# First feed-forward layer, token blocks 3 to 6: the first product as seven quarter products of 256 columns, with the work recorded and issued by a table of shifts

## The chip, the cores and the metric

The kernel runs on one core of a Trainium2 chip. The metric is the device time of one execution in microseconds (us); of several runs the median is given. The engines are named as in the profile: PE multiplies matrices, PEld is PE's loading of weights, DVE and ACT are the vector and the scalar engine, SP issues the DMAs.

## What is computed

Chunked attention over 4 sequences of 768 tokens and 8 heads of 64 gives 3072 rows of 512 numbers; two feed-forward layers follow. All of it is float32.

```python
# attention, per chunk of 32 tokens (8 memory tokens, 16 to the left, 8 to the right)
a = np.exp(scores - max);  out = (a / sum) @ v_full
x = out.transpose(0, 2, 1, 3).reshape(3072, 512)
h = np.maximum(x @ moe_w_in, 0.0)                 # 512 -> 2048
x = h * h @ moe_w_out                             # 2048 -> 512
h = x @ moe2_w_in                                 # 512 -> 2048
return (np.maximum(h, 0) + np.log1p(np.exp(-np.abs(h)))) @ moe2_w_out
```

## The kernel before

Every float32 operand of a large product is held as two parts, a high one (`xh`, `wh`, `gh`) and a low one (`xl`, `wl`, `gl`), and each product is three matmuls: low weights by high data, high by low, high by high.

The 3072 tokens are six blocks of 512 columns (`NB`; the code counts them from 0, the text from 1). The 2048 hidden units are 16 chunks of 128 (`KF`, index `f`); two chunks make a pair (`KP` = 8 pairs, index `p`). The program has three parts.

- **The head** (`FIRST`, an order written out by hand): loads, the attention of block 1, the splitting of the first layer's weights and block 1 of the first layer.
- **Blocks 2 to 6 of the first layer**: `step(n, f)`, called in the order of `n` and `f`. A step runs `h_mm` (12 matmuls of 512 columns into the PSUM tile `hp`: four pieces of the 512-long inner dimension by three parts), then `g_step` (ACT: relu, square, cast to `gh`; the low part `gl` follows on DVE, `act1_low`, at the next step), and `out_step` for a chunk two steps older (12 matmuls of 512 columns into the four accumulators `acc`). At the block's end `evac` copies the accumulators out and stores them (`x2s`). `x_split` makes `xh` and `xl` of the next block with four casts and four subtractions.
- **The second layer**: the blocks taken two at a time (`NGR` = 3 groups of 1024 tokens). Its first product is already made of seven products for every pair of weight chunks (`first_stage`), its second one is `second_stage`. Weights for it are prepared beforehand and kept in DRAM (`wa`, `wb`, `wo`).

Beside the matmuls, the steps of blocks 2 to 5 carry two other kinds of work. The attention of the next block is done in four pairs of units (`p_scores`, `p_exp`, `p_norm`, `p_squares`, `p_values`, `p_out`): short matmuls on PE, the softmax on DVE and ACT, 16 transposes of 32x32 tiles per pair of units on DVE. And `jobs2` splits the second layer's weights: `in_jobs` (load, join two 32-bit halves, four sums or differences, casts, stores to `wa` and `wb`) and `out_jobs` (the same without sums, to `wo`), one job per step.

All engines take their instructions in the order of the program, which here is the order in which the code is written (`tc.manual_schedule()`); SP's DMAs too stand in one queue in that order. A tile that is written anew waits for the last reader of what it held.

The lines of the before kernel that the prediction names:

```python
for a, b in ...:  matmul(out=hp, ...)         # L331, L332, L333: first product, three parts
nc.tensor.matmul(out=acc[m][:, cols], ...)    # L379: second product
nc.vector.transpose(pt[...], t[...])          # L240: transposes of the attention
nc.vector.tensor_tensor(out=o, in0=a, ...)    # L486: sums of second-layer weights, 256 columns
```

L278 and L171 are the attention's short matmuls, L309 makes `xl`, L355 makes `gl`, L436 and L437 join the halves of a second-layer weight, L294 is `p_out`'s copy out of PSUM, L343, L347 and L351 are relu, square and cast, L113 is the scaling of a weight's upper half, L423 is `store` (`wa`, `wb`).

Of the kernel before, what the change touches and what calls it, by code (L numbers as in the profile page):

```python
# [1 line left out]

# [30 lines left out]
UC = 2  # L33
# [12 lines left out]
NGR = NB // 2  # L46
SOFT_A = ((), (0,), (1,), (2, 3), (4,), (5,), (6, 7), ())
# [8 lines left out]
sc2 wb3 wd0 re1 wh0 mx2 cp0 wl2 wp0 vl4 mu1 wa3 va0 vl5 wd3 vl6 tr1 sb2 vl7 wh3 xh1 sc3 wp3 kl8 xh0 ex2 xl1 kl9 xl0  # L56
cp1 su2 va1 mx3 re2 xh2 sb3 wa1 mu2 ex3 wl3 wb1 tr2 xl2 xh3 su3 cp2 xl3 f10 wd1 re3 wh1 va2 mu3 wa2 wb5 wp1 tr3 xh5
cp3 xl5 wb2 xh4 va3 wd2 vl10 xl4 sc4 xh6 wl4 ra0 xl6 xh7 wh2 xl7 f11 wl5 wp2 vl9 mx4 wa5 f12 kl12 wb4 wa4 vl8 wd5
rb0 sb4 wh5 wd4 ra1 rc0 f13 wh4 ex4 wl6 wp4 rb1 kl10 su4 ra2 wb6 rb2 re4 wa6 rl0 f14 mu4 rc1 wd6 rc2 wa7 wb8 wh6 tr4
rl1 wb7 f20 cp4 wl7 wp6 kl11 ra3 vl11 wp5 va4 wa9 rl2 wa8 f21 wd7 rb3 wd8 f15 ra4 rb4 wb10 wh8 wb9 wb11 wh7 wl8 wd9  # L60
f22 wp8 wh9 xo9 xo8 wp7 rc3 wp9 wa10 sc5 rl3 rc4 wd10 f23 ra5 wa11 rl4 mx5 rb5 wd11 wh10 f24 sb5 wl9 wh11 wp10 ex5
wl10 wa12 su5 f16 wb12 re5 wd12 mu5 wh12 wb13 f17 ra6 wp11 wl11 wp12 wa14 tr5 wb14 f18 ra7 wd14 cp5 rb7 wa13 va5 rb6
wd13 rc7 vl14 f19 rc5 kl13 wh13 rl5 wb15 ra8 wl12 wp13 rc6 f25 xo10 xo11 rl6 wh14 ra9 wa15 sc6 f26 kl17 mx6 vl12
wd15 wl13 vl15 kl16 sb6 wh15 wp14 f110 rb8 wl14 wa16 vl13 rl7 kl14 kl15 ex6 rc8 f27 wa17 wb17 wb16 ra10 su6 rb10
f111 wd16 rl8 wh16 re6 wp15 rb9 f28 rc9 wd17 wa18 mu6 wb18 f112 rl9 wd18 wp16 tr6 f29 cp6 ra11 wh18 rb11 wp18 va6
rc11 f113 vl17 xo13 rc10 wl15 ra12 rl10 wh17 xo12 f210 wp17 rb12 sc7 wa19 f114 ra13 kl19 mx7 rc12 vl16 sb7 kl18 rl12
rl11 f115 wb19 ra14 rb13 wd19 rb14 wh19 f211 ra15 rc13 ex7 rl13 su7 f212 wp19 re7 mu7 tr7 f116 cp7 va7 ra16 rc14
f213 xo15 rl14 xo14 rb16 rb15 rc16 f214 rc15 rl15 rl16
# [3 lines left out]


@with_exitstack
def body(ctx: ExitStack, tc: tile.TileContext, qk, vW, w1, w2, out):
    nc = tc.nc
# [20 lines left out]
    raw, cf, wt = {}, {}, {}  # L97
# [31 lines left out]
    def w_h(layer, i, m=BOTH):  # L129
        if (layer, i) not in wt:  # L130
            t = wpool.tile([P, 2, 2, DM], F32R, tag=f"w{i}", name=f"w{layer}_{i}")
            wt[layer, i] = t[:, 0], t[:, 1]
        return nc.scalar.copy(out=wt[layer, i][0][:, m], in_=cf[layer, i, m.start])
# [45 lines left out]
    def p_max(n):  # L179
# [10 lines left out]
        m = at.tile([P, 2, PU * 2, 1], F32, tag="m", name="m", bufs=2)  # L190
# [41 lines left out]
    def p_squares(n, i):  # L232
# [137 lines left out]
    def out_mm(f, g, cols=ALL):  # L370
        gh, gl = g
        wh, wl = (a[:, 1] for a in wt[1, f])
        if f == 0 and cols.start == 0:
            for m in range(4):
                acc[m] = pa.tile([P, DM], F32, tag=f"acc{m}", name=f"acc{m}")
        for m in range(4):
            s = slice(m * P, (m + 1) * P)
            for j, (a, b) in enumerate(((wl[:, s], gh), (wh[:, s], gh), (wh[:, s], gl))):
# [22 lines left out]
    qk_s = wpool.tile([P, PU, NP, GQ + NK], F32, tag=f"w{KF - 1}", name="qk_s")  # L401
    v_s = wpool.tile([P, 2 * PU, UC, 2, 2, D], F32, tag=f"w{KF - 2}", name="v_s")
# [16 lines left out]
    wb = [dram.tile([P, 3, 2, QW], F32R, name=f"wb{p}") for p in range(KP)]  # L419
    wo = [dram.tile([P, 2, 2, DM], F32R, name=f"wo{p}") for p in range(KP)]  # L420
# [37 lines left out]

    def in_jobs(p):
# [13 lines left out]
        def split(k, x, *stores):  # L473
            t = cf_tile(k, (P, 2, 2, QW), F32R)
            halves(t[:, :, 0], t[:, :, 1], x, *[(o, t[:, i]) for o, i in stores], late=True)

        def sums():
            f = d["f"].rearrange("p i (h q) -> p i h q", h=2)
            s = d["s"] = cf_tile(0, (P, 4, QW))
            for out, a, b, op in (  # L480
                (s[:, 0], f[:, 1, 0], f[:, 1, 1], ALU.add),
                (s[:, 1], s[:, 0], f[:, 0, 0], ALU.subtract),
                (s[:, 2], f[:, 0, 1], s[:, 1], ALU.subtract),
                (s[:, 3], f[:, 0, 0], f[:, 1, 0], ALU.subtract),
            ):
                nc.vector.tensor_tensor(out=out, in0=a, in1=b, op=op)  # L486
# [8 lines left out]
        def at(fn, *a):  # L495
            return lambda: fn(*a)
# [390 lines left out]
```

## Time and profile before

| | |
|---|---|
| median of 3 runs | 1094.7 us (1093.49 to 1098.32) |
| the profiled execution | 1093.54 us |
| its span | 1091.7 us |
| granted TensorE clock | 1.00 throughout |
| PE busy | 1075.2 us (98% of the span) |
| PEld busy | 886.6 us (81%) |
| DVE busy | 709.3 us (65%) |
| ACT busy | 594.8 us (54%) |

The profiled execution's time is 1.8 us more than its span, the time from the first to the last instruction. PE's matmuls are pipelined, so a start-to-start distance, not the length of a record, says what one costs in a row.

### The profile page before, as it was taken

What the parts mean: (1) busy time and instruction counts of PE and PEld (TensorE: products, weight loads), DVE (VectorE), ACT (ScalarE), POOL (GpSimd) and SP (SyncE); (2) the same over time, 40 slices, a digit from 0 to 9 for tenths busy, and PEclk for the clock granted to TensorE, in tenths of its full rate; (3) what the DMA queues carried; (4) which work ended last, traced back from release to release, by engine and by line L of the source; (5) the groups of instructions that cost most, each with busy time, mean ns of one, the idle gap of its engine ahead of it and who ended that gap; (6) DMA issues with size and microseconds to landing.
All of it is one profiled execution on the core that took longest, in us unless ns stands there. A gap on an engine that the chain in (4) does not pass through costs nothing.

```text
span 1091.7 us, 18550 instructions
## 1 busy us (share of the span) xinstructions
PE 1075.2 (98%) x7592; PEld 886.6 (81%) x7592; DVE 709.3 (65%) x1175; ACT 594.8 (54%) x926; POOL 0.7 (0%) x6
## 2 busy tenths in 40 slices
PE   5999999999999999999999999999999999999998
PEld 4888888888888888888888888888888888888886
DVE  6876576666667665764332788952788952788822
ACT  3876444454454554546445767732767732767522
POOL 0000000000000000000000000000000000000000
PEclk9999999999999999999999999999999999999999
DMA  9774242354445254534512656234556334555202
GB/s 354 276 281 155 90 165 103 124 202 155 152 160 181 98 176 162 183 113 157 181 39 93 239 189 257 99 126 150 185 183 258 111 118 154 183 187 219 77 1 77
DMA packets 49428, 174.99 MB, mean 160 GB/s; under 512 B 5312, under 2 KB 5312, under 8 KB 41152
## 3 DMA queue, kind: packets, MB, share of 16 engines
q1 hardware_dynamic: 49344, 173.82, 45.2%
q8 instruction: 59, 0.97, 0.4%
q14 instruction: 25, 0.20, 0.1%
HBM read 138.15 MB, written 35.65 MB: 159 GB/s over the span
## 4 chain that ended last, share of the span: by engine, by line
PE 95%; DMA 2%; DVE 1%; ACT 1%; issue 0%; SPq 0%; ACTq 0%
PE acc L379 23%; PE bk L807 23%; PE bk L724 21%; PE hp L331 8%; PE hp L332 8%; PE hp L333 8%; PE xs L278 1%; DMA qk<-qk 1%; PE xs L171 1%; PE xp L278 1%; DMA x2f<-x2s 1%; PE sc L171 1%; DMA r<-w 1%; PE xpe L278 0%; PE pp L254 0%
## 5 line engine op out<-in xcount | busy, mean ns | idle before, releaser
L379 PE MATMUL acc<-gh,w 128*128 128x512 f32 (+1 forms) x776 | 238.1, 388 | 0.0
L807 PE MATMUL bk<-ws,gh 128*128 128x512 f32 x768 | 236.5, 389 | 0.0
L724 PE MATMUL bk<-xo,ws 128*128 128x512 f32 x1008 | 230.2, 389 | 0.0
L724 PEld LDWEIGHTS bk<-xo,ws 128*128 128x128 f32 x1008 | 189.0, 188 | 39.9 <-DVE h L768 0.8
L379 PEld LDWEIGHTS acc<-gh,w 128*128 128x128 f32 x776 | 144.5, 188 | 29.8
L807 PEld LDWEIGHTS bk<-ws,gh 128*128 128x128 f32 x768 | 144.2, 188 | 30.1
L331 PE MATMUL hp<-xh,w 128*128 128x512 f32 (+1 forms) x388 | 153.3, 395 | 0.0
L332 PE MATMUL hp<-xl,w 128*128 128x512 f32 (+1 forms) x388 | 151.0, 389 | 0.0
L333 PE MATMUL hp<-xh,w 128*128 128x512 f32 (+1 forms) x388 | 150.9, 389 | 0.0
L379 PE MATMUL acc<-gl,w 128*128 128x512 f32 (+1 forms) x388 | 150.1, 387 | 0.0
L807 PE MATMUL bk<-ws,gl 128*128 128x512 f32 x384 | 149.5, 389 | 0.2 <-DVE gl L444 0.2
L355 DVE TENSOR_TENSOR gl<-r,gh 128x512 fp32r<-128x512 f32 (+1 forms) x97 | 66.2, 684 | 97.2 <-ACT gh L351 96.8
L444 DVE TENSOR_TENSOR gl<-h,gh 128x512 fp32r<-128x512 f32 x96 | 66.1, 689 | 83.7 <-ACT gh L449 83.4
L449 ACT CAST gh<-h 128x512 fp32r<-128x512 f32 x96 | 59.3, 621 | 106.9 <-PE bk L807 106.7
L343 ACT ACTIVATE r<-hp 128x512 f32<-128x512 f32 (+1 forms) x97 | 57.4, 592 | 105.3 <-PE hp L333 99.9
L331 PEld LDWEIGHTS hp<-xh,w 128*128 128x128 f32 x388 | 73.4, 189 | 15.7
L333 PEld LDWEIGHTS hp<-xh,w 128*128 128x128 f32 x388 | 73.4, 189 | 15.1
L332 PEld LDWEIGHTS hp<-xl,w 128*128 128x128 f32 x388 | 73.4, 189 | 14.4 <-DVE xl L321 0.2
L379 PEld LDWEIGHTS acc<-gl,w 128*128 128x128 f32 x388 | 72.8, 188 | 14.8
L807 PEld LDWEIGHTS bk<-ws,gl 128*128 128x128 f32 x384 | 72.1, 188 | 15.6 <-DVE gl L444 0.8
L240 DVE STREAM_TRANSPOSE pt<-t 32x128 f32<-32x128 f32 x256 | 77.5, 303 | 4.3
L347 ACT ACTIVATE r<-r 128x512 f32<-128x512 f32 (+1 forms) x97 | 60.8, 629 | 2.6
(79 smaller groups left out, 1087.9 us busy)
## 6 DMA issues: line engine op xcount, KB each, us to landing
ws<-wa SPq DMA_DIRECT2D x24, 1024.0 KB, 6.4
ws<-wo SPq DMA_DIRECT2D x24, 1024.0 KB, 4.9
ws<-wb SPq DMA_DIRECT2D x24, 768.0 KB, 4.3
r<-w SPq DMA_DIRECT2D x16, 1024.0 KB, 7.2
cf<-w SPq DMA_DIRECT2D x32, 512.0 KB, 5.3
qk<-qk SPq DMA_DIRECT2D x46, 336.0 KB, 5.4
v<-vW SPq DMA_DIRECT2D x44, 256.0 KB, 5.3
wo<-cf SPq DMA_DIRECT2D x16, 512.0 KB, 2.9
```

Source lines behind the costliest of these rows:

```text
L240: nc.vector.transpose(pt[b:b + 32, g], t[g * 32:(g + 1) * 32, i, h])
L331: nc.tensor.matmul(out=hp, lhsT=b, rhs=xh[:, c], start=(c == 0), stop=False)
L332: nc.tensor.matmul(out=hp, lhsT=a, rhs=xl[:, c], start=False, stop=False)
L333: nc.tensor.matmul(out=hp, lhsT=a, rhs=xh[:, c], start=False, stop=(c == KD - 1))
L343: nc.scalar.activation(out=r, in_=hp, func=AF.Relu)
L347: nc.scalar.activation(out=r, in_=r, func=AF.Square)
L355: nc.vector.tensor_tensor(out=gl, in0=r, in1=gh.bitcast(F32), op=ALU.subtract)
L379: nc.tensor.matmul(out=acc[m][:, cols], lhsT=a, rhs=b, start=(f == 0 and j == 0 and cols.start == 0), stop=(f == KF - 1 and j == 2),)
L444: nc.vector.tensor_tensor(out=lo, in0=x, in1=hi.bitcast(F32), op=ALU.subtract)
L449: nc.scalar.copy(out=hi, in_=x)
L724: nc.tensor.matmul(out=bk, lhsT=a, rhs=b, start=(start and n == 0), stop=(n == 5), skip_group_check=not start)
L807: nc.tensor.matmul(out=bk, lhsT=a, rhs=b, start=(f == 0 and j == 0), stop=(f == KF - 1 and j == 2))
```

## The change

In blocks 3 to 6 (code `n` = 2 to 5) the first product of a pair of chunks takes the form that the second layer has. The block's 512 columns are two halves of 256, the inner dimension is two halves, the pair of chunks is two; instead of eight products of such quarters there are seven, of sums and differences of the quarters. A product (`quarter`) is 6 matmuls of 256 columns. So a pair takes 7 x 6 = 42 matmuls of 256 columns where it took 24 of 512.

What this needs:

- **Weights.** `sum_jobs` makes, in block 2, four sums of the first layer's weights for each pair, splits them and stores them in DRAM (`wx`, 8 x 4 x 256 KB). `sum_load` brings each of the four back into a fixed place in SBUF once for every pair and block (tiles named `w_9`, `w_11`, `w_13`, `w_15`), after its last reader.
- **Data.** `octet` makes four differences and seven split parts (`xe`, and two in the tiles `w_1` to `w_7`) of each block, where `x_split` made four parts.
- **PSUM.** A pair has one tile `hq` with two halves `e` and `a`. Seven results pass through them and are put together in SBUF (`r`) by four ACT copies and three DVE additions of 256 columns per pair, where ACT read `hp` directly. Relu, square, cast and low part stay.
- **Place of the jobs.** `jobs1` (the sums) take `in_jobs`' place in block 2; `in_jobs` go to blocks 3 to 5, `out_jobs` to block 6, where the data for the second layer (`x_jobs`) is made too.
- **Buffers.** `qk` has 2 buffers instead of 4, `m` and `s` one each. The head's loads of `qk` stand elsewhere in `FIRST`. The second layer's first weights (`ws`) go to other places, and the last two `out_step`s stand behind the first two products of the second layer.
- **Order.** From block 2 to the second pair of the second layer nothing is issued as the code is written. A `Recorder` keeps every instruction; `play` puts each DMA, DVE and ACT instruction at its place among PE's instructions, moved by a number from the table `MOVES`, and issues all in that order. Where two tiles share a buffer, `play` adds a dependency so that they take it in the order of issue.

```diff
+MOVES = (
+    """
+19 34 39 2 8 17 -56 -8 -56 3 22 26 28 30 33 40 45 49 34 41 46 50 -42 -45 1 4 3 7 3 6 3 6 -1 1 4 10 11 18 23 27 12 20
...
+    def play(self, moves):
+        jobs, self.jobs = self.jobs, None
...
+            if engine is self.nc.tensor:
+                order.append((at + 0.5, i))
+                at += 1
+            else:
+                order.append((at + int(next(moves, 0)), i))
+        for _, i in sorted(order):
...
-            t = at.tile([P, NP, GQ + NK], F32, tag="qk", name="qk", bufs=2 * PU)
+            t = at.tile([P, NP, GQ + NK], F32, tag="qk", name="qk", bufs=PU)
...
+        def words():
+            f = d["f"] = cf_tile(ka)
+            for i in range(2):
+                hi, lo = (a[:, 0].bitcast(F32) for a in wt[1, 2 * p + i])
+                nc.vector.tensor_tensor(out=f[:, i], in0=hi, in1=lo, op=ALU.add)
...
+        def casts():
+            split(kc, d["s"][:, 0:2], (wx[p][:, 0:2], slice(0, 2)))
+            split(ka, d["s"][:, 2:4], (wx[p][:, 2:4], slice(0, 2)))
...
+        def sum_place(i):
+            return whole[9 + 2 * i][:, :, 0, 0:QW]
+
+        def sum_load(p, i):
+            store(sum_place(i), wx[p % KP][:, i])
...
+        def quarter(x, w, bk, start):
+            n = 0
+            for k in range(2):
+                wh, wl = (w[:, h, k * P:(k + 1) * P] for h in range(2))
+                for a, b in ((wl, x[0][:, k]), (wh, x[1][:, k]), (wh, x[0][:, k])):
+                    nc.tensor.matmul(out=bk, lhsT=a, rhs=b, start=(start and n == 0), stop=(n == 5), skip_group_check=not start)
...
+            if old:
+                on, op, oe, oa, or0, or1 = old
+                quarter(xp_o[on, 2], sum_place(1), oa, False)
+                quarter(xp_o[on, 3], sum_place(2), oe, False)
+                if here:
+                    for i in (1, 2):
+                        sum_load(op + 1, i)
+            outs(1)
+            if old:
+                nc.scalar.copy(out=or0[:, half[1]], in_=oa)
+                nc.vector.tensor_tensor(out=or0[:, half[1]], in0=oe, in1=or0[:, half[1]], op=ALU.add)
+                nc.scalar.activation(out=or0, in_=or0, func=AF.Relu)
+            if here:
+                bk = ps.tile([P, BLK], F32, tag="ps", name="hq")
+                e, a = bk[:, half[0]], bk[:, half[1]]
+                quarter(xp_o[n, 4], whole[2 * p][:, :, 0, QW:], e, True)
...
+                quarter(xp_o[on, 5], sum_place(3), oa, False)
...
-            for n in range(1, NB):
-                for f in range(KF):
-                    step(n, f)
+            for f in range(KF):
+                step(f)
...
+            for n in range(2, NB):
+                for p in range(KP):
+                    slot(n, p)
```

A pair's work is spread over three calls of `slot`: the first product of quarters and two more in its own, three in the next (`old`), the last one there too, and its relu, square and second product in the next and the one after it. Recorded instructions all carry the line L157, so the rows below are told apart by their tiles.

**PE, in a middle block.** Before, one step: the last matmuls of a first product (`hp`) and the second product of a chunk two steps older (`acc`).

```order
L331 MATMUL hp<-xh,w_6_905 128x512
L332 MATMUL hp<-xl,w_6_905 128x512
L333 MATMUL hp<-xh,w_6_905 128x512
L379 MATMUL acc_3851<-gh,w_4_705 128x512 x2
L379 MATMUL acc_3851<-gl,w_4_705 128x512
L379 MATMUL acc_3852<-gh,w_4_705 128x512 x2
L379 MATMUL acc_3852<-gl,w_4_705 128x512
```

After, in block 3, from the third quarter of one pair (`w_11`) to its fifth (`w_15`), with the first quarter of the next pair (`w_6`) between:

```order
L157 MATMUL hq<-xe,w_11_1160 128x256 x6
L157 MATMUL hq<-xe,w_13_1351 128x256 x6
L157 MATMUL acc_1768<-gh,w_2_603 128x512 x2
L157 MATMUL acc_1768<-gl,w_2_603 128x512
L157 MATMUL hq<-xe,w_6_914 128x256 x6
L157 MATMUL acc_1770<-gh,w_2_603 128x512 x2
L157 MATMUL acc_1770<-gl,w_2_603 128x512
L157 MATMUL acc_1764<-gh,w_3_670 128x512 x2
L157 MATMUL acc_1764<-gl,w_3_670 128x512
L157 MATMUL hq<-w_1_469,w_15_1452 128x256
```

The first product no longer stands in one run of 12; its quarters alternate with pieces of the second product, and a half of `hq` is read and written again after some 18 to 21 matmuls.

**DVE, in a middle block.** Before, the softmax of a pair of attention units, with its first eight transposes in one run:

```order
L191 TENSOR_REDUCE m<-xs 128x8
L197 TENSOR_TENSOR t<-xs,m 128x512
L211 TENSOR_REDUCE s<-t 128x8
L216 TENSOR_SCALAR s<-s 128x8
L217 RECIPROCAL s<-s 128x8
L221 TENSOR_TENSOR t<-t,s 128x512
L240 STREAM_TRANSPOSE pt<-t 32x128 x8
L355 TENSOR_TENSOR gl<-r,gh 128x512
```

After, in block 3, the same work (`m`, `t`, `s`, `pt`), with additions out of PSUM (`r<-hq,r`), a low part (`gl`) and work on second-layer weights (`cf`) in it:

```order
L157 TENSOR_TENSOR cf<-cf 128x256 x3
L157 TENSOR_REDUCE m<-xs 128x8
L157 TENSOR_TENSOR t<-xs,m 128x512
L157 TENSOR_TENSOR gl<-r,gh 128x512
L157 TENSOR_REDUCE s<-t 128x8
L157 TENSOR_TENSOR r<-hq,r 128x256
L157 TENSOR_SCALAR s<-s 128x8
L157 RECIPROCAL s<-s 128x8
L157 TENSOR_TENSOR t<-t,s 128x512
L157 TENSOR_TENSOR cf<-cf 128x2x256
L157 STREAM_TRANSPOSE pt<-t 32x128 x5
L157 TENSOR_TENSOR r<-hq,r 128x256
```

The additions that PE waits for now stand between the softmax's steps, behind a reduction that itself waits for ACT.

**SP, in a middle block.** Before, the loads of a pair of attention units among the stores of a pair of weights:

```order
L423 DMA wb_101<-cf 128x1024
L423 DMA wa_93<-cf 128x512
L155 DMA v<-vW 128x512
L148 DMA qk<-qk 128x672
L423 DMA wa_93<-cf 128x1024
L423 DMA wb_101<-cf 128x512
```

After, the same stores with the reloads of the weight sums (`<-wx`) between them:

```order
L157 DMA w_9_1066<-wx_111 128x2x256
L157 DMA v<-vW 128x512
L157 DMA wb_101<-cf 128x1024
L157 DMA qk<-qk 128x672
L157 DMA wa_93<-cf 128x512
L157 DMA w_11_1160<-wx_111 128x2x256
L157 DMA w_13_1351<-wx_111 128x2x256
L157 DMA wa_93<-cf 128x1024
L157 DMA w_15_1452<-wx_111 128x2x256
```

A reload stands behind stores that wait for DVE's low parts.

## Rows read from the trace of the kernel before

**Rows 1.** The page, part 1: busy time of each engine over the span.
```profile
PE 1075.2 (98%) x7592; PEld 886.6 (81%) x7592; DVE 709.3 (65%) x1175; ACT 594.8 (54%) x926; POOL 0.7 (0%) x6
```

**Rows 2.** The chain that ended last: shares, then pieces: start us, us, what.
```profile
PE 95%; DMA 2%; DVE 1%; ACT 1%; issue 0%; SPq 0%; ACTq 0%
...
215.21 5.44 PE acc L379 x24
...
310.81 5.44 PE acc L379 x24
```

**Rows 3.** What PE waited for: us in total, times, longest.
```profile
PE sc L171 <- DMA qk<-qk: 5.8, 2, 4.6
...
PE bk L807 <- DVE gl L444: 0.2, 1, 0.2
```

**Rows 4.** Busy time by stretch: us, PE, PEld, DVE, ACT, POOL, PEclk, DMA share, GB/s.
```profile
119.60:215.21 95.61, 95.61 (x898) 78.60 (x897) 62.62 (x144) 45.67 (x82) 0.00 (x0) 1.00 0.40 134
215.21:310.81 95.60, 95.60 (x897) 78.58 (x897) 63.26 (x145) 48.19 (x86) 0.00 (x0) 1.00 0.45 154
406.41:502.01 95.60, 95.60 (x897) 78.58 (x897) 62.37 (x139) 49.80 (x89) 0.00 (x0) 1.00 0.46 155
502.01:598.50 96.49, 96.49 (x427) 79.89 (x427) 34.67 (x55) 48.98 (x84) 0.00 (x0) 1.00 0.30 105
```

**Rows 5.** PE in order of time, two first products one behind the other: start us, us.
```profile
322.53 0.39 PE L331 MATMUL hp<-xh,w 128*128 128x512 f32 x1
...
327.74 0.39 PE L333 MATMUL hp<-xh,w 128*128 128x512 f32 x1
327.97 0.62 PE L379 MATMUL acc<-gh,w 128*128 128x512 f32 x2
```

**Rows 6.** The same in the head, where block 1's first chunk runs in 256 columns.
```profile
31.36 0.28 PE L332 MATMUL hp<-xl,w 128*128 128x256 f32 x1
...
32.66 0.40 PE L331 MATMUL hp<-xh,w 128*128 128x512 f32 x1
...
44.21 0.28 PE L379 MATMUL acc<-gl,w 128*128 128x256 f32 x1
...
45.41 0.40 PE L331 MATMUL hp<-xh,w 128*128 128x512 f32 x1
```

**Rows 7.** DVE by shape: count, busy us, mean ns of one, idle before.
```profile
L240 DVE STREAM_TRANSPOSE pt<-t 32x128 f32<-32x128 f32 x256 | 77.5, 303 | 4.3
L355 DVE TENSOR_TENSOR gl<-r,gh 128x512 fp32r<-128x512 f32 x95 | 65.4, 690 | 97.2 <-ACT gh L351 96.8
L436 DVE TENSOR_SCALAR cf<-cf 128x512 uint32<-128x512 uint32 x32 | 13.6, 426 | 17.6 <-DMA cf<-w 17.2
L486 DVE TENSOR_TENSOR cf<-cf 128x256 f32<-128x256 f32 x32 | 12.9, 422 | 0.6
L309 DVE TENSOR_TENSOR xl<-xf,xh 128x512 fp32r<-128x512 f32 x20 | 12.5, 686 | 15.8 <-ACT xh L308 15.8
```

**Rows 8.** ACT by shape, the same columns.
```profile
L347 ACT ACTIVATE r<-r 128x512 f32<-128x512 f32 x95 | 59.9, 633 | 2.6
L351 ACT CAST gh<-r 128x512 fp32r<-128x512 f32 x95 | 59.0, 622 | 3.2 <-PE acc L379 0.5
L113 ACT ACTIVATE cf<-cf 128x512 f32<-128x512 f32 x32 | 21.6, 676 | 49.1 <-DMA cf<-w 43.8 <-DVE cf L444 5.0 <-issue 0.2
L294 ACT COPY xf<-xs 128x256 f32<-128x256 f32 x24 | 7.8, 375 | 24.1 <-PE xs L171 24.1
```

**Rows 9.** Busy time in the second layer's first stage, columns as in rows 4.
```profile
622.00:670.00 48.00, 48.00 (x213) 39.77 (x212) 42.78 (x48) 35.50 (x46) 0.00 (x0) 1.00 0.56 198
```

**Rows 10.** What SP's DMA queue waited for, columns as in rows 3.
```profile
SPq L423 <- DVE cf L444: 217.6, 35, 16.1
```

**Rows 11.** DMA issues: count, KB each, median us from issue to landing.
```profile
wb<-cf SPq DMA_DIRECT2D x8, 256.0 KB, 3.4
```

More of the change, by code (lines that the diff above doesn't have):

```diff
@@ L59 @@
[L59 to L63, printed above, removed]
@@ L479, in sums, with casts @@
             s = d["s"] = cf_tile(0, (P, 4, QW))
[L480 to L486, printed above, removed]
+            four(s, f)
+        def casts():
+            f = d["f"].rearrange("p i (h q) -> p i h q", h=2)
             split(1, f[:, :, 1], (wb[p][:, 0:2], slice(0, 2)))
@@ L561, in split @@
             halves(t[:, 0, k], t[:, 1, k], d["x"][i], late=(grp == 0))
[L563 removed]
+        return [lambda: sums(0), lambda: sums(1)] + [lambda i=i: part(i) for i in range(7)]
     with tc.manual_schedule(engines={mybir.EngineType.SP}):
@@ L633, in body, with run, take, step @@
                 pending.append((0, products[i][0], (gh, gl), ALL))
-        def step(n, f):
+        def run(jobs):
+            for job in jobs:
+                job()
+        def take(jobs):
+            return jobs.pop(0) if jobs else ((), (), (), ())
+        def step(f):
+            pair = 2 * PB + f // 4
             if f == 0:
@@ new lines, in octet, with add, part @@
+        def octet(n, *what):
+            xf = xf_t[1, n]
+            b11, b12, b21, b22 = (xf[:, 2 * (j // 2):2 * (j // 2) + 2, half[j % 2]] for j in range(4))
+            sums = {"t1": (b12, b12, b11), "t2": (b22, b22, b12), "t3": (b11, b22, b11), "t4": (b21, b21, b22)}
+            src = b11, b12, b22, b22, b21, b11, b21
+            def add(t):
+                o, a, b = sums[t]
+                nc.vector.tensor_tensor(out=o, in0=a, in1=b, op=ALU.subtract)
+            def part(i):
+                hi, lo = xp_o[n, i] = octet_tile(n, i)
+                halves(hi, lo, src[i])
+            return [(lambda w=w: add(w)) if isinstance(w, str) else (lambda w=w: part(w)) for w in what]
@@ new lines, in activate, with row @@
+        def activate(item, r):
+            nc.scalar.activation(out=r, in_=r, func=AF.Square)
+            gh, gl = g_tiles()
+            nc.scalar.copy(out=gh, in_=r)
+            rest.append((gl, r, gh))
+            pending.append((*item, (gh, gl)))
+        life, ready, visited, rows = [], [], [], [0]
+        def row():
+            rows[0] += 1
+            if rows[0] % 4:
+                return tmp("r")
+            return (late[0] if late else at).tile([P, BLK], F32, tag="r", name="r", bufs=1)
@@ new lines, in slot @@
+            run(e1[3])
+            outs(1)
+            if here and n == NB - 1:
+                run(plan.get(2 * p, ()))
+            visit("mid")
+            flush()
+            run(e2[0])
+            at_point(3)
+            if here:
+                quarter(xp_o[n, 1], sum_place(0), e, True)
+                if (n, p) != (NB - 1, KP - 1):
+                    sum_load(p + 1, 0)
+                quarter(xp_o[n, 0], whole[2 * p][:, :, 0, 0:QW], a, False)
+            outs(2)
+            show_up()
@@ new lines, in slot @@
+            if here:
+                r1 = row()
+                nc.scalar.copy(out=r1[:, half[1]], in_=e)
+                nc.vector.tensor_tensor(out=r0[:, half[0]], in0=a, in1=r0[:, half[0]], op=ALU.add)
+            run(e2[1])
+            at_point(4)
+            run(e2[2])
+            run(e2[3])
+            if here and n == NB - 1:
+                run(plan.get(2 * p + 1, ()))
+            if old:
+                quarter(xp_o[on, 6], whole[2 * op + 1][:, :, 0, QW:], oa, False)
+                ready.append(((on, 2 * op + 1), oa, or1))
@@ L692, in body @@
+            if here:
+                life.append((n, p, e, a, r0, r1))
+            visit("end")
+            outs(len(todo))
+            if n == NB - 1 and p > 5:
+                for _ in range(2 if p == 7 else 1):
+                    fetch()
+        late_ctx = []
+        places = [([xpool], "xl"), ([xpool], "xh"), (late, "r1"), (late, "r0"), (late, "r2"), ([wpool], f"w{KF - 1}")]
         loads = []
```

398 lines of the change are left out of this document (287 added, 111 removed), and 47 rows, old and new, of the table MOVES.

## The prediction, written before the run

> **What bounds the kernel now.** I read four views in this order. The page's first part has PE busy 98% of the span, DVE 65%, ACT 54% [rows 1]; records of matmuls overlap, so that alone does not say that PE sets the end. The chain of waits does: 95% of it is PE, and its pieces return every 95.60 us, once a block [rows 2]. PE's own waits: the longest kind is 5.8 us, in the head, and on DVE the second layer has 0.2 us; none falls in blocks 2 to 6 [rows 3]. Last the stretches: in blocks 2, 3 and 5 DVE works 62 to 63 of 95.6 us and ACT 46 to 50, in block 6 DVE 34.67 and ACT 48.98 of 96.49 [rows 4]. So where the change works the end moves by what PE issues, plus any wait that PE gets.
>
> **PE's matmuls.** 24 matmuls of 512 columns start between 322.53 and 327.97 us: 5.44 / 24 = 0.2267 us each [rows 5]. Of 256 columns the head has two runs: eleven starts from 31.36 to 32.66 us, 0.1182 each, and ten from 44.21 to 45.41, 0.120 each [rows 6]. Half the columns so cost 0.52 to 0.53 of the time; I take 0.1185, since the first run is, as here, a first product. Four blocks of 8 pairs lose 32 x 24 = 768 of the long ones, 768 x 0.2267 = 174.1 us, and get 32 x 42 = 1344 short ones, 159.3 us. That is **14.8 us less** on PE (15.2 to 12.8 between the two runs). The attention's matmuls keep their number and their five visits a block, so 95.60 - 16 x 5.44 = 8.56 us a block stays. A block with attention becomes 8 x (42 x 0.1185 + 24 x 0.2267) + 8.56 = 91.9 us, block 6 83.3 us.
>
> [...]
>
> **What DVE and ACT get.** PE's gain is kept only where they keep up, on shorter blocks. Block 3 after the change, counted in the program's order: 64 transposes (x 0.303), 64 instructions of 512 elements (14 `gl`, 16 of the softmax, 14 for the next quarters' operands, 20 for second-layer weights; x 0.69), 39 of 256 (22 additions out of PSUM, 17 weight sums; x 0.42), 8 scalings (x 0.43), 1.5 us of small ones [rows 7]. That is 19.4 + 44.2 + 16.4 + 3.4 + 1.5 = 84.9 us. Means overlap when instructions follow closely: 20 of 686 ns make 13.7 us, and 12.5 were busy [rows 7]. So 77 to 85 of 91.9 us, 84 to 92%, where it was 66%. Block 4 has 2 us less, block 5 only 63 us, since no weight jobs are left. Block 2, with first-layer sums for the later blocks in place of `in_jobs`, has 84.6 of 95.6.
>
> In block 6 ACT is the full one: 32 copies of 256 (x 0.375), 34 relus and squares (x 0.63), 17 + 33 casts (x 0.62), 15 scalings (x 0.676), 8 others (x 0.62), together 79.4 of 83.3 us by means [rows 8], 95%.
>
> What such a share costs PE, the trace shows once: from 622 to 670 us DVE was busy 42.78 of 48 us, 89%, and PE waited for nothing there [rows 9]. That is the lower bound, **no wait**. It is a stage with long instructions and PE results that may wait, though. The new form has short slack. Between the last matmul of an attention visit and the fifth quarter (`w_15`) PE has 15 matmuls of 512 and 18 of 256, 5.53 us. Before that quarter DVE and ACT have to do, in order: max 0.69, copy out 0.375, subtract 0.69, second copy 0.375, exp 0.63, sum 0.69, addition 0.42 = 3.87 us [rows 7, 8]. The addition stands behind the softmax's sum, and that behind ACT's exp. Spare: 1.66 us. Ahead of the chain in DVE's queue stand a weight's joins and sums, ten instructions of 5 to 6.5 us. If they end more than 1.66 us after the visit, PE pays the rest. Following the queues by hand through the first four and a half pairs of block 3 I come to about 3 us of waits, 0.65 a pair: 0.8 at the block's start, where eleven instructions for the quarters' operands stand in a row, and 1.5 at this place. Over blocks 3 and 4 that is the upper bound, 16 x 0.65 = 10.4 us; block 6 on ACT gives 0 to 8 x 0.65 = 5.2. Where PE is late once, the next pairs have more slack; and the one measured stretch of this share is without waits. So I take half of the bound for blocks 3 and 4, **5.2 us**, and **1 us** for block 6.
>
> **The rest.** The head's `qk` loads stand elsewhere, and its waits are on them [rows 3]: -1 to +1 us, taken as 0. The first two products of the second layer stand ahead of the last two second products, and cover the last pair's chain of relu, square, cast and low part, 0.63 + 0.63 + 0.62 + 0.69 = 2.6 us [rows 7, 8], with 12 x 0.2267 = 2.7 us and more matmuls between: taken as 0, up to 1 if that cover fails. Half as many `qk` buffers: the load is due a visit later, some 25 us, and costs no wait. PE's weight loads: one per matmul before and after, hidden in the 256-column runs too, since the starts of rows 6 have them in.
>
> **The sum**, against the profiled execution's own time, 1093.5 us (span 1091.7 + 1.8; it lies 1.2 us under the median): 1093.5 - 14.8 + 5.2 + 1 = 1084.9, **1085 us**. Low end: 1093.5 - 15.2 - 1 = 1077. High end: 1093.5 - 12.8 + 10.4 + 5.2 + 1 = 1097. A difference under 0.5% (5.5 us, against the median 1094.7: 1089.2 to 1100.2) is about what a measurement of this kernel cannot tell from no change.
>
> **The rivals.**
> 1. *No wait*: the order of the table holds as it does at 89% in the second layer [rows 9]. Time 1093.5 - 14.8 = 1079, between 1077 and 1080. For it: many DVE instructions (weights) need not be on time. Against it: the spare of 1.66 us above. 20%.
> 2. *DVE becomes the bound* in blocks 3 and 4 and ACT in block 6: the full 10.4 + 5.2 us come back, 1093.5 - 14.8 + 15.6 = 1094, between 1089 and 1099: no difference. For it: 84 to 92% is a mean over blocks, single pairs have more. Against: rows 9. 22%. [...]
> 3. *SP's queue makes it slower.* Four reloads of weight sums a pair stand in one queue with the stores of second-layer weights. A reload may start when its last reader is done and is read again a pair later: 10.4 - 0.7 = 9.7 us, less 3.4 to land [rows 11], leaves 6.3. Such stores held the queue 35 times, 6.2 us on average and up to 16.1 [rows 10]. If the longer half, about 10 us, hits once per weight pair and PE waits 10 - 6.3 = 3.7 us for each of the 8, that is 30 us: 1093.5 - 14.8 + 30 = 1109. It decides from 20.3 us of waits on, 0.63 a pair. For it: a DVE that is nearly full ends those low parts late, and the stores stand directly ahead of the reloads of `w_11`, `w_13` and `w_15`. Against: in the kernel before the stores were queued long before their results, with nothing behind them in a hurry, so that those 6.2 us are no lateness. 14%.
>
> That the change doesn't do what it says is no rival: the order has 768 long matmuls fewer and 1344 short ones more.
>
> **How the numbers follow.** The forecast's own case (1080 to 1089) has 44%, and no wait 20%: faster by over 0.5% 64%. Within 0.5%: 22%. Slower: 14%. The range 1077 to 1097 holds the first two cases and most of the third.
>
> **What would show it.** Right: 42 starts of 0.118 to 0.120 us a pair, with no gap where the long and the short ones meet; blocks 3 to 5 of 92 to 95 us and block 6 of 84 to 85; PE's waits on DVE (`r`, `gl`) and ACT (`r`) together some 6 us, most in blocks 3 and 4 at the quarter behind a visit, few in block 5. No wait would show block 3 at 91.9; rival 2 a DVE without idle time there and block 3 over 93.5. Rival 3 would show PE waiting for DMA on `w_9` to `w_15`. The forecast is wrong if the short matmuls cost more among the long ones than in a run of their own, which no row here shows, or if waits gather in block 2 or at the second layer's start.

## The result, and the profile after

The changed kernel takes **1107.0 us** (median of 4 runs, 1105.4 to 1112.3), the kernel before 1094.1 beside it: a ratio of 1.0113, interval 1.0082 to 1.0144. It is slower by 1.1%; 1085 was forecast and the range ended at 1097. The profiled execution took 1107.4 us, with a span of 1105.4, 13.7 more than before.

First the page's part 1 and the shares of the chain of waits, which answer to [rows 1, 2], and four pieces of that chain from block 3 (start us, us, what):

```profile
PE 1073.3 (97%) x8168; PEld 902.8 (82%) x8168; DVE 785.9 (71%) x1365; ACT 649.3 (59%) x1084; POOL 0.7 (0%) x6
...
PE 78%; DMA 13%; DVE 5%; ACT 2%; issue 1%; SPq 0%; DVEq 0%; ACTq 0%
...
266.41 4.74 DMA wa<-cf
271.21 1.04 DMA cf<-w
...
274.54 5.30 DMA cf<-w
...
289.24 0.70 DVE gl L157
```

PE had 95% of the chain and now has 78%; DMA went from 2 to 13%. The transfers in it are not the reloads of sums. They belong to the second layer's weights: `cf<-w` brings raw weights into a `cf` tile, `wa<-cf`, `wb<-cf` and `wo<-cf` store the finished halves out of one, and the next load into that tile waits for the store.

What PE waited for from block 3 to the second layer, columns as in [rows 3], where these kinds of wait did not exist:

```profile
PE acc L157 <- ACT gh L157: 4.4, 3, 2.4
PE hq L157 <- DVE r L157: 4.3, 6, 2.1
PE acc L157 <- DVE gl L157: 3.3, 5, 1.5
PE hq L157 <- ACT r L157: 2.1, 2, 1.1
PE hq L157 <- DMA w<-wx: 0.8, 1, 0.8
```

That is 14.9 us, and not all: a matmul's record lasts longer than the distance to the next start (0.40 us on the mean against 0.2267 for 512 columns, 0.28 against 0.120 for 256), so the start of a wait hides in it. I count **pauses** from the starts instead: whatever a matmul starts later than 0.2267 us (512 columns) or 0.120 us (256) after the one before, less the same count of the kernel before, where the attention's visits make up nearly all of it. Block 3 has 6.5 us, block 4 has 9.0, block 5 0.8, block 6 with the second layer's start 9.6, the rest 0.4: **26.3 us**. Saving and pauses come from the same starts, so together they must give the change of the span, and they do: 768 x 0.2267 = 174.1 us went, 1344 x 0.120 = 161.3 came, 12.8 less; 1091.7 - 12.8 + 26.3 = 1105.2, and the span is 1105.4.

The blocks, from the first quarter of one to that of the next, columns as in [rows 4]; the last stretch is most of block 6:

```profile
217.06:315.20 98.14, 94.72 (x1038) 81.69 (x1037) 78.47 (x188) 59.60 (x123) 0.00 (x0) 1.00 0.77 256
315.20:416.50 101.30, 95.49 (x1041) 82.47 (x1040) 77.30 (x183) 61.38 (x126) 0.00 (x0) 1.00 0.76 245
416.50:509.60 93.10, 93.10 (x1041) 82.93 (x1040) 59.96 (x145) 51.64 (x105) 0.00 (x0) 1.00 0.53 159
509.60:600.00 90.40, 84.43 (x504) 73.10 (x503) 57.70 (x107) 62.57 (x125) 0.00 (x0) 0.98 0.90 297
```

Block 5 is what was forecast. Blocks 3 and 4 are 6 and 9 us longer than 8 x (42 x 0.120 + 24 x 0.2267) + 8.56 = 92.4 us, with DVE busy 78 of 98 and 77 of 101 us, so it had time over. What stands out is the DMA share: 0.76 to 0.90 in the three stretches with pauses (in blocks 3, 4 and 6 of the kernel before it was 0.45, 0.50 and 0.30) and 0.53 in the one without.

One pause as it comes about, in block 3. SP's issues, DVE and PE (start us, us, instruction, count, in brackets the idle time before it):

```profile
266.41 0.33 SPq L157 DMA_DIRECT2D wa<-cf  x1
266.84 1.56 SPq L157 DMA_DIRECT2D w<-wx  x2
271.21 0.34 SPq L157 DMA_DIRECT2D cf<-w  x1
...
272.93 0.69 DVE L157 TENSOR_TENSOR cf<-cf 128x512 fp32r<-128x512 f32 x1
275.78 0.43 DVE L157 TENSOR_SCALAR cf<-cf 128x512 uint32<-128x512 uint32 x1 [2.16 <-issue]
276.12 0.68 DVE L157 TENSOR_TENSOR gl<-r,gh 128x512 fp32r<-128x512 f32 x1
...
279.94 0.44 DVE L157 TENSOR_SCALAR cf<-cf 128x512 uint32<-128x512 uint32 x1 [2.79 <-DMA cf<-w]
...
274.77 0.62 PE L157 MATMUL acc<-gh,w 128*128 128x512 f32 x2
276.86 0.50 PE L157 MATMUL acc<-gl,w 128*128 128x512 f32 x1 [1.47 <-DVE gl L157]
```

The store `wa<-cf` of 512 KB is in flight together with two reloads, the DMA engines 90% busy, and lands 4.74 us later, at 271.15 (the median of such stores from 215 to 602 us is 4.0 us, 2.7 in the kernel before). Only then can `cf<-w` be issued into its tile, at 271.21, and it lands at 275.70. DVE's next instruction is the first on that load, so DVE stands still from 273.62 to 275.78. Behind it in the queue is the `gl` that PE needs, and PE stands too. The profile names no releaser for this one stop ("issue"); that it ends 0.08 us after the landing says what it was. The next one, of 2.79 us at 279.94, the profile puts to `cf<-w` itself (issued at 274.54, landed at 279.84).

The view by tile gives the sum of the stops that the profile puts to `cf<-w`, on DVE and ACT together, from 215 to 602 us (us, times), first for the changed kernel, then for the kernel before:

```profile
its engine sat idle before it (us, times) until:
  DMA cf<-w: 64.8, 34
...
  DMA cf<-w: 50.3, 16
```

The 34 stops take 0.2 to 4.0 us each, and a late load can stand in the sum twice, once on DVE and once on ACT. The kernel before had 50.3 us of this in 16 stops, and none of them reached PE. So a sum of stops does not yet say what they cost.

### The profile page after: what moved, and what is told of

It reads as the page before. It is cut to its first block, busy times and chain, and to the rows that moved or that the text cites. A ratio compares the mean times of both kernels' runs of the same rounds, so it can differ in the third digit from the quotient of the medians.

```text
span 1105.4 us, 20436 instructions
## 1 busy us (share of the span) xinstructions
PE 1073.3 (97%) x8168; PEld 902.8 (82%) x8168; DVE 785.9 (71%) x1365; ACT 649.3 (59%) x1084; POOL 0.7 (0%) x6
## 4 chain that ended last, share of the span: by engine, by line
PE 78%; DMA 13%; DVE 5%; ACT 2%; issue 1%; SPq 0%; DVEq 0%; ACTq 0%
PE bk L1172 24%; PE bk L1084 19%; PE acc L157 12%; PE hq L157 7%; DMA cf<-w 6%; PE hp L157 4%; PE acc L480 3%; DMA wo<-cf 2%; DVE cf L157 2%; PE xs L157 2%; DMA wa<-cf 2%; PE bk L157 1%; PE hp L433 1%; PE hp L434 1%; PE hp L435 1%
## 5 line engine op out<-in xcount | busy, mean ns | idle before, releaser
L157 PE MATMUL acc<-gh,w 128*128 128x512 f32 x656 | 207.5, 398 | 4.4 <-ACT gh L157 4.4
L157 PEld LDWEIGHTS hq<-xe,w 128*128 128x128 f32 x1056 | 141.0, 190 | 17.1 <-DVE r L157 3.7
L157 PE MATMUL hq<-xe,w 128*128 128x256 f32 x1056 | 146.2, 284 | 5.4 <-DVE r L157 2.5
L157 PE MATMUL acc<-gl,w 128*128 128x512 f32 x328 | 129.5, 395 | 3.6 <-DVE gl L157 3.3
L157 PEld LDWEIGHTS acc<-gh,w 128*128 128x128 f32 x656 | 112.3, 190 | 20.9 <-ACT gh L157 6.8
L157 ACT ACTIVATE r<-r 128x512 f32<-128x512 f32 x144 | 91.1, 633 | 21.7 <-DVE r L157 19.3
L1172 PEld LDWEIGHTS bk<-ws,gl 128*128 128x128 f32 x384 | 72.1, 188 | 15.6 <-DVE gl L549 0.6
L157 DVE STREAM_TRANSPOSE pt<-t 32x128 f32<-32x128 f32 x256 | 77.5, 303 | 4.3
L157 PEld LDWEIGHTS acc<-gl,w 128*128 128x128 f32 x328 | 61.8, 189 | 22.4 <-DVE gl L157 8.7
L157 ACT COPY r<-hq 128x256 f32<-128x256 f32 x128 | 47.1, 369 | 51.6 <-PE hq L157 49.5
L157 DVE TENSOR_TENSOR gl<-r,gh 128x512 fp32r<-128x512 f32 x80 | 55.0, 688 | 27.9 <-ACT gh L157 26.8
L157 DVE TENSOR_TENSOR cf<-cf 128x256 f32<-128x256 f32 (+2 forms) x129 | 66.0, 540 | 10.3 <-ACT cf L157 6.3
L1095 DVE SCALAR_TENSOR_TENSOR h<-h,cf 128x1024 f32<-128x1024 f32 x47 | 57.3, 1219 | 1.1 <-ACT cf L1092 1.1
L1094 DVE TENSOR_TENSOR cf<-cf 128x1024 f32<-128x1024 f32 x47 | 57.3, 1220 | 0.5
L1096 DVE TENSOR_TENSOR h<-h,cf 128x1024 f32<-128x1024 f32 x47 | 57.3, 1219 | 0.5
```

The costliest lines, as they stand in the source:

```text
L157: ins = job().ins
L1094: nc.vector.tensor_tensor(out=c, in0=z, in1=c, op=ALU.subtract)
L1095: nc.vector.scalar_tensor_tensor(out=h, in0=h, scalar=0.0, in1=l, op0=ALU.max, op1=ALU.add)
L1096: nc.vector.tensor_tensor(out=h, in0=h, in1=c, op=ALU.add)
L1172: nc.tensor.matmul(out=bk, lhsT=a, rhs=b, start=(f == 0 and j == 0), stop=(f == KF - 1 and j == 2))
```

## The experiments

Three theories. **A**: the reloads make the second layer's transfers late, DVE and ACT stop at them in order, PE waits behind. **B**: DVE and ACT are simply too full (rival 2). **C**: a bank of quarters turns round too tightly, so each stop reaches PE. "Stops" is the row just shown (in a3 and c3, whose block 6 ends later, up to its end), "pauses" the count from the starts, and a dash in the landings means that there is none. Pauses hold the time that is lost at the lower granted clock too: from block 3 on it is 0.50 in place of 1.00 for 34 us in c3, 24 in d1, 17 in a3, 14 in c1 and 3 in the changed kernel, c4 and d2 (its means over the whole span, head included: 0.982, 0.987, 0.991, 0.989, 0.998, 0.994 and 0.995); in the changed kernel these 3 us come right behind PE's longest pause.

| kernel | us | ratio to before (95%) | `cf<-w` lands in | stops, us (times) | pauses, us |
|---|---|---|---|---|---|
| kernel before | 1094.1 | 1 | 5.3 | 50.3 (16) | 0 |
| changed kernel | 1107.0 | 1.0082 to 1.0144 | 6.1 | 64.8 (34) | 26.3 |
| a1: sums loaded once | 1093.0 | 0.9967 to 0.9994 | 5.1 | 28.5 (19) | 8.8 |
| a2: reloads of 16 rows | 1095.1 | 0.9987 to 1.0023 | 5.5 | 39.5 (23) | 12.3 |
| a3: reloads on GpSimd | 1117.2 | 1.0197 to 1.0234 | 6.5 | 68.3 (26) | 33.8 |
| b1: before, less PE | 1080.5 | 0.9862 to 0.9892 | 5.2 | 57.4 (16) | 0 |
| c1: b1 with copies | 1120.2 | 1.0185 to 1.0254 | 7.0 | 152.6 (23) | 36 |
| c2: no loads `cf<-w` | 1087.7 | 0.9918 to 0.9959 | - | 0 | 4.7 |
| c3: as recorded | 1153.0 | 1.0487 to 1.0582 | 5.8 | 27.0 (14) | 73.7 |
| c4: fewer transposes | 1104.4 | 1.0060 to 1.0104 | 6.0 | 62.7 (31) | 21.0 |
| d1: first new table | 1164.3 | 1.0593 to 1.0663 | 5.5 | 2.0 (1) | 75.3 |
| d2: second new table | 1091.4 | 0.9954 to 0.9989 | 6.0 | 13.4 (8) | 8.1 |
| d3: third new table | 1088.7 | 0.9932 to 0.9970 | 5.9 | 5.1 (5) | 7.0 |
| e1: d3, sums loaded once | 1085.7 | 0.9904 to 0.9944 | 5.5 | 0.4 (1) | 2.6 |

**a1, a2, a3: the reloads.** In a1 a reload after the first of its place uses up its shift and issues nothing; a2 moves 16 of 128 rows; a3 changes the queue. The edits in that order (`...` where lines are left out):

```diff
+            if job is None:
+                continue
...
     store(sum_place(i), wx[p % KP][:, i])
+    if i in loaded:
+        nc.drop()
+    loaded.add(i)
```

```diff
-    store(sum_place(i), wx[p % KP][:, i])
+    rows = slice(0, 16 if i in loaded else P)
+    loaded.add(i)
+    store(sum_place(i)[rows], wx[p % KP][rows, i])
```

```diff
-    store(sum_place(i), wx[p % KP][:, i])
+    nc.gpsimd.dma_start(out=sum_place(i).bitcast(F32), in_=wx[p % KP][:, i].bitcast(F32))
```

> The changed kernel without its reloads: the four sums of the first pair are loaded once, and the 124 later loads of 256 KB are left out (so the sums of pair 0 are used in every pair); every other instruction stands where it stood. Theory A (the reloads hold up the second layer's weight jobs: they stand in SP's queue behind PE and fill the DMA engines, so that VectorE and ScalarE stop at late cf<-w and PE waits for them): the 26.6 us of waits that PE has in blocks 3 to 6 fall to about 6, so 1086 us, 1081 to 1092. Theory B (VectorE and ScalarE have too little idle time beside a shorter first product, whatever the DMAs do): no load is on its path, 1102 to 1108. Theory C (a bank of quarters turns round too tightly, each stop of VectorE or ScalarE reaches PE): the stops at cf<-w are as many as before the change, 1100 to 1108.

> The changed kernel with every reload after the first of its place cut to 16 of 128 partitions (32 KB for 256 KB), so that the queue of SP keeps each reload and its wait for PE, and the DMA engines lose 29 MB; the other 112 rows of a sum keep those of pair 0. Theory A by traffic: 1086 to 1092, like the kernel without reloads. Theory A by SP's order (a reload that waits for PE stops what is queued behind it): 1102 to 1108. Half and half gives about 1097. Theories B and C: 1100 to 1108.

> The changed kernel with all 128 loads of sums issued by GpSimd in place of SP: the same bytes, but what waits for PE no longer stands ahead of cf<-w, wa<-cf and wo<-cf. Theory A by SP's order: 1086 to 1095. Theory A by traffic: 1102 to 1110, or more if GpSimd's issue of a load is slow. Theories B and C: 1100 to 1108.

Without reloads the kernel is 14 us faster, and the stops fall to 28.5 us. Theory B is out as the main cause, since DVE's work is untouched. But a1 is not back at 1086, and lies just above theory A's range: 8.8 us of pauses stay. A part of the rest is none of the reloads' doing: in a1's profile block 3 begins at 221.5 in place of 217.1 us, and in its head, from 30 to 40 us, the mean granted clock is 0.66, where the changed kernel's is 1.00. The pauses, which leave the head out, fell by 17.5 us. a2 says that the bytes did it: with each reload and its wait for PE still in SP's queue, 12 of those 14 us are gone, and a1 and a2 differ by 2 us, about their intervals (1095.1 is nearer to "half and half" than to the range for traffic alone, so a small part for SP's order is not excluded). a3 is against SP's order from the other side: with no reload waiting for PE in SP's queue the kernel is 10 us slower still. Two queues take 41.2% and 29.7% of the 16 DMA engines' time from 215 to 602 us then, where the changed kernel's one queue takes 73.2%, and `cf<-w` lands in 6.5 us in place of 6.1. Part of the loss is the clock: block 3 of a3 has a granted clock of 0.95 on the mean (the number before the DMA share), where the changed kernel has 1.00. Why the stops grew is open.

```profile
218.54:323.08 104.54, 98.32 (x1039) 85.58 (x1037) 79.31 (x189) 60.98 (x125) 22.66 (x32) 0.95 0.74 245
```

**b1, c1: the form of before.** b1 leaves out one matmul of twelve in each first product of blocks 3 to 6; c1 adds two copies of 256 KB a step to it (the tiles `extra` that they go to are left out here).

```diff
-nc.tensor.matmul(out=hp, lhsT=a, rhs=xl[:, c], start=False, stop=False)
+if blk < 2 or c != 1:
+    nc.tensor.matmul(out=hp, lhsT=a, rhs=xl[:, c], start=False, stop=False)
```

```diff
+if n >= 2:
+    for i in range(2):
+        nc.sync.dma_start(out=extra[(2 * f + i) % 4][:, :, 0:DM // 4], in_=w1[2 * (f % 4) + i][:, 0:DM // 2].rearrange("p (i q) -> p i q", i=2))
```

> The kernel before with one of the twelve matmuls of each first product of blocks 3 to 6 left out (64 x 0.2267 = 14.5 us of TensorE, about what the change saves); VectorE, ScalarE and the DMAs keep the work and the order of before. If the other engines of the kernel before can follow a shorter TensorE (theory A wants that): 1094 - 14.5 = 1080 us, up to 1084. Theory B: they cannot, and the waits come here too: 1088 to 1095. Theory C: no quarters here, so 1080.

> The kernel before with one matmul of twelve left out of each first product of blocks 3 to 6 (1080.5 us so far), and with 128 more transfers of 256 KB in SP's queue, two a step in these blocks, which wait for no engine (they copy a part of the first weights to memory that nobody reads). If traffic of that size is enough to bring the waits, whatever the first product looks like: PE waits 14 to 20 us, 1094 to 1101. If it takes the quarters and the packed second-layer jobs of the change for the traffic to hurt: 1080 to 1085, with cf<-w landing later than in the kernel without the copies but no PE wait.

b1 gives back all of its 14.5 us, 1094.6 - 1080.5 = 14.1, with 57.4 us of stops and no pause. So the stops were there before the change (50.3 us) and cost nothing; the old form has room for them. That is a part of theory C: in a1, with 28.5 us of stops, fewer than before the change, the form of quarters still pauses for 8.8 us. c1 takes 40 us more than b1, where at most 21 were expected: traffic of the size of the reloads is enough to stop a kernel that has no quarters. It is a hard form of it, though. The copies stand ahead of each step's loads, and SP also waited 27.2 us for copies to land before it could issue the next, so the 40 us are not the price of the traffic alone.

**c2, c4: which of the late things, and DVE's load.** The first edit is c2's, for the loads of `out_jobs` (those of `in_jobs` get the same), the second c4's, which stands behind the transposes of the softmax.

```diff
-nc.sync.dma_start(out=t, in_=w2[f][:, DM:])
+nc.gpsimd.memset(t.bitcast(F32), 0.0)
```

```diff
+if n >= 3 * PB and i > 0:
+    nc.drop()
...
+        nc.gpsimd.memset(pt[i * 32:i * 32 + 32], 0.0)
```

> The changed kernel with the 32 loads cf<-w of 512 KB in blocks 3 to 6 left out (GpSimd fills the tile with zeros in their place, so the second layer's weights are wrong); all 128 reloads, the stores and every other instruction stay. Theory A (the reloads hurt through the loads cf<-w, at which VectorE and ScalarE stop in order): most of the waits go, 1087 to 1095. If the reloads hurt by being late themselves, or through the stores: 1100 to 1108.

> The changed kernel with 12 of the 16 transposes on VectorE left out of each of the twelve visits of blocks 3 to 5 (GpSimd fills their place with zeros, so three quarters of the softmax weights are wrong): 12 x 12 x 0.303 = 43.6 us less for VectorE, 14.5 a block; the DMAs and the order of everything else stay. Theory B (VectorE's load is the bound in blocks 3 and 4): of the 15.5 us that PE waits in these two blocks beyond the kernel before, 10 or more go, and block 6 is left as it is, 1092 to 1098. Theory A (late loads): VectorE stops at cf<-w as before and only catches up sooner, 1101 to 1107.

c2 keeps all 128 reloads, and the pauses fall to 4.7 us. What PE waits for there, from 215 to 662 us:

```profile
PE hq L157 <- ACT r L157: 0.5, 2, 0.3
PE acc L157 <- ACT gh L157: 0.4, 1, 0.4
```

With every reload in place, and none of them late for PE, most of the pauses go with the loads at which DVE and ACT stop. 17 MB of traffic went as well, so c2 has less of the cause along with less of the path. c4 takes 43.6 us of work from DVE and gains 2.6, less than the intervals can tell from nothing; the stops stay at 62.7. In blocks 3 and 4 some 5 us of pauses went, where theory B wanted 10 or more: with less work DVE catches up sooner behind a stop, but its load is not the bound.

**c3: the table.** Every shift is zero (`order.append((at, i))`).

> The changed kernel with every shift of the table at zero: the seven quarters, the reloads and all jobs stay, issued where the code writes them. If the table's order is itself what makes VectorE and ScalarE stop ahead of PE's work, this is faster than 1107 us, 1090 to 1105. If the table only repairs a part of what the quarters bring: slower, 1110 to 1140, with more PE waits of the same kinds.

In the order of the code the kernel takes 1153 us, more than any case expected: the table of the change is worth 46. It is not the table as such that loses, then. The stops are down to 27.0 us here, and PE waits 27.9 us on additions out of the quarters' bank instead.

**d1, d2, d3: the same work in another order.** If A is right, the fault is where the jobs stand that need a late load. So only the numbers of the table were changed (and read as fractions, to order jobs between two matmuls). I took them from a model of the in-order queues and the shared DMA engines, with durations from the traces:

```diff
-order.append((at + int(next(moves, 0)), i))
+order.append((at + float(next(moves, 0)), i))
```

> The changed kernel with another table: the same instructions, tiles, bytes and matmul order; only the places of the jobs of VectorE, ScalarE and SP between the matmuls differ. The places come from a queue model of this stretch whose durations and landings are those of the changed kernel's trace (a DMA system of about 300 GB/s behind one queue, with which it gives the changed kernel's waits), searched for an order in which what needs a late load stands behind what PE needs next, also at 255 to 310 GB/s. Theory A (PE waits only because the jobs of the late cf<-w loads stand ahead of its own in the queues): 16 to 20 us of the 26.6 go, with the traffic unchanged, 1088 to 1093. Theory B (VectorE's load is the bound): the order cannot help, 1102 to 1108. If the DMA traffic costs PE directly, by late reloads or by more conflicts: 1098 to 1108.

> Another table for the changed kernel, the same instructions, bytes and matmul order. The first such table took away the stops at late loads (5.5 us in place of 64.8) and was slower all the same, since in its queues PE's next quarter stood ready before ScalarE had copied out the other half of the same PSUM bank, and the program orders the two (PE hq after ACT r: 38 waits, 25.3 us). This table comes from the same queue model with that order added: PE, VectorE and ScalarE take turns on a bank, whichever half they use, and a result costs 0.43 us from a copy to PE, 0.73 from a 512-column VectorE instruction. The model gives the changed kernel 507.7 us for this stretch (505.9 measured), the first table 542.8 (555.5) and this one 487.4 to 487.7 at 280 to 330 GB/s. Theory A (late loads hurt only through the order of the queues) and the bank's turns: 20 us less than the changed kernel, 1087 us, 1084 to 1094. If the traffic itself costs PE: 1098 to 1108. If the model misses another wait, as the first time: over 1110.

> The second table, searched on with the same model under harder conditions (235 to 300 GB/s, results up to 0.22 us later, instructions up to 9% longer), so that there is room around the places that wait by little; instructions, bytes and the order of the matmuls are unchanged. The second table left PE 4.1 us of pauses in blocks 3 to 6 and 2.7 at the second layer's start. Expected: 1088 to 1091 us, 1 to 3 us under the second table, if room is what was short; 1091 to 1094 if those pauses come from things the model has not in it.

d1 did what it was made for, the stops went from 64.8 to 2.0 us, and it is 57 us slower than the change, where 14 to 19 less were expected. What PE waited for in d1, from 215 to 662 us (the expectation of d2 counts from 119 to 640 us):

```profile
PE hq L193 <- ACT r L193: 27.1, 40, 2.9
PE hq L193 <- DVE r L193: 7.8, 7, 2.7
PE xs L193 <- ACT xf L193: 5.3, 7, 1.7
```

Two quarters lie in the two halves of one `hq` tile, their bank, and the program as built lets the engines use a bank only in turn, whichever half they touch (the first row: 40 waits, 27.1 us): PE's quarter into one half waits for ACT's copy out of the other, and that copy for DVE's addition. My model had them apart, and its order put them next to each other. With these turns in it the model gives 542.8 us for the stretch of d1 (555.5 measured), and the order made from it, d2, is 15.6 us faster than the changed kernel. From d2's profile, DVE at the same weight as in the pause above, then PE's waits, and the landings (count, KB, median us):

```profile
273.21 0.69 DVE L192 TENSOR_TENSOR gl<-r,gh 128x512 fp32r<-128x512 f32 x1 [1.44 <-ACT gh L192]
274.05 0.42 DVE L192 TENSOR_TENSOR r<-hq,r 128x256 f32<-128x256 f32 x1
274.51 0.62 DVE L192 STREAM_TRANSPOSE pt<-t 32x128 f32<-32x128 f32 x2
275.16 0.43 DVE L192 TENSOR_SCALAR cf<-cf 128x512 uint32<-128x512 uint32 x1
...
PE bk L192 <- DMA ws<-wa: 1.8, 1, 1.8
PE hq L192 <- DMA w<-wx: 0.7, 1, 0.7
...
w<-wx SPq DMA_DIRECT2D x124, 256.0 KB, 4.6
cf<-w SPq DMA_DIRECT2D x30, 512.0 KB, 6.0
wo<-cf SPq DMA_DIRECT2D x16, 512.0 KB, 6.0
```

The loads land as late as in the changed kernel (6.0 and 6.1 us), and hardly anyone stands at them (13.4 us of stops in place of 64.8): here the load was issued at 268.60 in place of 271.21 us and the instruction on it comes behind `gl`, `r` and some transposes, at 275.16, when the load is there. So the table moves the loads as well as what consumes them; from a load's issue to DVE's first instruction on it the mean is 6.9 us in the changed kernel and 9.2 in d3. Which of the two moves it takes is not shown. In block 4 it also takes some 5 us of DVE's work out, into block 5 (72.0 us busy in d3 in place of 77.3), so the clean case is block 3, with the same work on DVE and the same DMA share. d3, with more room at the near places, takes 1088.7 us, **0.5% under the kernel before** (0.3 to 0.7), and is the fastest complete kernel of these runs. Its block 3 is 92.2 us long, 0.3 from the forecast, with DVE busy 78.8 us (78.5 in the changed kernel) and a DMA share of 0.81 (0.77):

```profile
220.31:312.48 92.17, 92.17 (x1038) 82.33 (x1037) 78.84 (x186) 61.14 (x125) 0.00 (x0) 1.00 0.81 261
```

**e1: the traffic under the better order.** d3 with the edit of a1.

> The kernel with the third table, and the 124 reloads after the first left out as in the run with the sums loaded once (so pair 0's sums serve all pairs). With the table of the change this saved 14 us. Theory A (the traffic costs only through the order of the queues): with an order that suits the late loads it saves next to nothing, 0 to 2 us. If the traffic costs PE in another way too: 4 us or more.

The reloads cost 14 us under the table of the change and 3.0 under this one, between the two expectations and with intervals of 2 us on each side (the pauses fall from 7.0 to 2.6). Most of their price came from the order in which their traffic met the jobs; that the rest is zero is not shown.

## Why the prediction was wrong, point by point

- **PE's matmuls**, a term of the right kind and 2 us too large: 12.8 us less where 14.8 stood in the sum, the low end of its bounds. I had taken the first run of [rows 6]; in the blocks twelve quarters' matmuls start from 271.23 to 272.67 us, 0.120 each, as in the second run:

```profile
271.23 1.60 PE L157 MATMUL hq<-xe,w 128*128 128x256 f32 x12
272.67 0.63 PE L157 MATMUL acc<-gh,w 128*128 128x512 f32 x2
```

  No gap where long and short ones meet, as said.
- **What DVE and ACT get: the step that failed.** The waits were put at 5.2 + 1 us, at most 15.6, and were 26.3. The chain of 3.87 us against 5.53 took every input of DVE and ACT as there on time, but for the softmax. With the loads out of the way (c2) 4.7 us of pauses stay, and 2.6 to 8 in the orders that go round them, which is of the size of the forecast 6.2; that they come from that chain is not shown, since the profile names only 0.9 us of waits in c2. No term priced what the reloads do to other transfers, though [rows 10] showed SP's queue full of second-layer stores and the page's list of issues showed its loads. The missing term is the stop at a `cf<-w`: 34 of 0.2 to 4.0 us, 64.8 us in all, 20 of them longer than the 1.66 us of spare that I had worked out. With the reloads away (a1) 28.5 us of them are left and 8.8 of pauses; with an order that goes round them (d3) 5.1 and 7.0.
- **"Many DVE instructions (weights) need not be on time"**, my reason for rival 1, is the error in one sentence. PE does not wait for a weight's join; but in a queue that is served in order everything behind it waits with it: in the pause above DVE stood 2.16 us at a join, `gl` behind it, and PE 1.47 us at `gl`.
- **[rows 9]**, 89% of DVE without a wait, was a poor witness: between 622 and 670 us no wait of DVE or ACT is on a load.
- **Rival 2** fell: DVE was 80% busy in block 3 and 76% in block 4, and c4 gained 2.6 us. ACT, which was to be the full one in block 6 (95% by means), was busy 62.6 of 90.4 us there. That 256 elements take DVE 422 ns, where half of the 690 for 512 is 345 [rows 7], was not what decided either.
- **Rival 3** had the size, 1109, by luck, and the cause in part: the reloads, SP and the second-layer weights. The path was the reverse. The stores were to make the reloads late; PE waited for a reload once, 0.8 us. The reloads made the stores and loads late, and the waits showed up on DVE and ACT.
- **The rest.** Head, blocks 2 and 5 and the second layer's steady part came out as said. Block 6 with the boundary, put at 1 us, lost 9.6: three `cf` tiles take turns there, each with a load of 6.1 and a store of 6.3 us (2.9 in b1), at DMA engines 90% busy. The reloads are not all of that: without them (a1) the stores still take 5.5 us.
- One more cost, a part of those 9.6 us, had no place in the sum: behind PE's longest pause (2.6 us at 541 us) the granted clock is 0.50 in place of 1.00 for 3.4 us, which the row of 520 to 550 us has as 0.94:

```profile
520.00:550.00 30.00, 26.47 (x150) 22.11 (x149) 16.55 (x31) 18.44 (x37) 0.00 (x0) 0.94 0.98 327
```

## What to carry to other kernels

Where a change adds transfers, ask which other transfers share the DMA engines with them, and which instruction stands at the head of an in-order queue when those come late; the wait then shows on an engine that has nothing to do with the new bytes (here 64.8 us on DVE and ACT at `cf<-w`, and 0.8 us on PE at a reload). A stop that costs nothing in one order (57.4 us of them in b1) can cost PE a good part of its length in the next (2.16 us on DVE were 1.47 on PE in block 3), so after shortening an engine's work, compare the spare time behind each stop with the stop's length, and leave more time between a load's issue and the first instruction on it. An order tuned by numbers is worth as much as the model behind it: here the orders made without and with the bank's turns take 1164 and 1091 us.

## What the runs showed that I had not expected

- Two engines on two halves of one bank of quarters take turns by the program's own waits: 40 waits and 27.1 us of PE on ACT's copies in d1. Whether the chip needs them, no run here shows.
- Moving 128 loads from SP's queue to GpSimd's, where nothing else waits, made the kernel 10 us slower (a3). A part of it is a lower granted clock, 0.95 in block 3; the rest stays open.
- 50 us of stops on DVE and ACT cost the kernel before nothing, and 57 us cost nothing in b1, while orders of the changed kernel with 2.0 and 27.0 us of stops are the slowest (d1, c3). Idle time, even much of it, says little until one knows what stands behind it.
